# An attention and expert kernel: scatters of three batches in groups of three, gating operations moved behind the step's maximum

## The chip, the cores and the metric

The kernel runs on one core of a Trainium2 chip. The metric is the device time of one execution in microseconds (us). The core has five queues that run beside each other, each in its own program order: TensorE (PE; its weight loads are shown as PEld), VectorE (DVE), ScalarE (ACT), GpSimd (POOL) and the DMA issue of SyncE (SP). They wait for each other by semaphores.

## What is computed

Eight batches of 576 tokens go through an attention of eight heads (four with a local mask of 32, four with a strided one). The result, 4608 tokens of 512 numbers, goes through a layer of eight experts of which each token uses the one with the largest logit.

```python
scores = np.where(masks, scale * q @ k.T, -1e9)
attn = exp(scores - max) / (sum + 1e-9)
x = (attn @ v).transpose(0, 2, 1, 3).reshape(4608, 512)

logits = x @ w_gate
e_idx = np.argmax(logits, axis=1)
probs = softmax(logits)
gate_w = probs[np.arange(N), e_idx]
eom = 1.0 / (1.0 + np.exp(-(x @ w_output_gate)))
for e in range(E):
    mask = e_idx == e
    h = np.maximum(x[mask] @ w1[e], 0.0)
    out[mask] = gate_w[mask, None] * eom[mask, e, None] * (h @ w2[e])
```

## The kernel before

There are two stages. The attention stage has 40 steps, five for each batch, numbered t = 0 to 39, and then a tail (the second loop of `attention`) that drains what is left. The order on every queue is the order in which the program writes the instructions; nothing is reordered.

A step is a software pipeline over several step indices at once. In order: the scores of step t (`scores`, TensorE, L261 and L266), the normalisation of step t-4 in three parts (`norm`, VectorE, L347, L349, L352, whose result is x_t), the copy of turned rows of step t-5 (`evac_x`, ScalarE, L392 to L402), the rows' transfers to memory (`rows`, SP), the mask added (`bar`, VectorE, L279 or L284), the turned probabilities of step t-2 (`turn_p`, TensorE, L319) and their copy (`evac_p`, ScalarE, L325), the value matmuls of step t-3 (`values`, TensorE, L334 or L337), the row maximum (`top`, VectorE, L293), its subtraction (`shift`, GpSimd, L308), the turned rows of step t-4 (`turn_x`, TensorE, L383) and the exponential (`expo`, ScalarE, L312). The PSUM tiles of scores, of turned probabilities and of values have one buffer each.

Between these lie eight places, `pump(1)` to `pump(8)`: the first ahead of the second part of the normalisation, the second ahead of its third part, the third and fourth behind the maximum, its subtraction and the turned rows, the fifth to eighth behind the exponential. At each place every running chain puts out one further operation. A chain is a generator: `yield n` skips n places, and `yield 0, p` waits for place p. In the tail the places have no numbers, and a chain puts out its operations until one yields more than 0.

Each batch b has one chain for the second half of its logits, and at its end `gating`: the largest logit and its column `oh`, the sum of the exponentials (L550), the output logit of the chosen expert (L528, L531) and its sigmoid (L553, ScalarE), the slot numbers of the tokens (`numbers`, TensorE, L536 to L541; L592 and L595, VectorE), the count so far (`cum`, L589), and the gate weight (L597, L599, L602). Then come six scatters (L609, GpSimd), of 96 rows of 64 bytes each, into the `table` from which the experts' tokens are read. For batches 0 to 5 (`steady`) the chain lies in steps 5b+11 to 5b+13; batches 6 and 7 are gated in the tail. The scatters of batches 0 to 2 (`ci < EB - 1`, where EB is 4) begin two steps later. Behind the gating of batch 3 a chain `pick` (L453 to L466) chooses the first expert, and `ahead` loads its weights and gathers its first tokens.

The second stage runs the eight experts one behind another, on TensorE (L853, L873).

Of the kernel before, what the change touches and what calls it, by code (L numbers as in the profile page):

```python
# [34 lines left out]
EB = 4  # L35
# [20 lines left out]
def attn_moe_kernel(  # L56
# [21 lines left out]
    def distinct(ins, group):  # L78
        for other in group:
            tc.declare_no_dep(ins.ins, other.ins, reason="rows of one scatter are no rows of another")  # L80
        group.append(ins)
# [90 lines left out]
    def attention():  # L172
        with ExitStack() as actx:
# [276 lines left out]
            def pick():  # L450

                cp = ps_g.tile([128, 512], F32, name="gp")
                nc.tensor.matmul(out=cp[:, 0:E], lhsT=tri[0:QB, 1, :], rhs=cum[0:QB, EB, :], start=True, stop=True)  # L453
                yield 1
                nc.vector.scalar_tensor_tensor(out=pk[:, 0, :], in0=cp[:, 0:E], scalar=float(E), in1=wts,
                                               op0=ALU.mult, op1=ALU.add)
                yield 0
                nc.vector.tensor_reduce(out=pick_f, in_=pk[:, 0, :], axis=AX.X, op=ALU.max)
                yield 0
                nc.vector.tensor_tensor(out=first, in0=pk[:, 0, :], in1=pick_f.to_broadcast([128, E]), op=ALU.is_equal)  # L460
                yield 0
                nc.vector.tensor_tensor(out=pk[:, 1, :], in0=first, in1=eidx, op=ALU.mult)
                yield 0
                nc.vector.tensor_reduce(out=pick_f, in_=pk[:, 1, :], axis=AX.X, op=ALU.add)
                yield 0
                nc.vector.tensor_copy(out=pick_i, in_=pick_f)  # L466
# [47 lines left out]
            def gating(b, j0, j1, ci):  # L514
                n = j1 - j0
                steady = ci < HALVED - 1
# [10 lines left out]
                def output_logit():  # L527
                    V.tensor_tensor(out=dd[:, 2], in0=oh, in1=l[:, :, E:2 * E], op=ALU.mult)  # L528

                def output_sum():  # L530
                    R(out=f[:, 3, :], in_=dd[:, 2], axis=AX.X, op=ALU.add)  # L531

                def numbers():
                    pp_ = ps_g.tile([128, 512], F32, name="gp")
                    pv = pp_[0:QB, 0:n * E]
                    nc.tensor.matmul(out=pv, lhsT=tri[0:QB, 0, 0:QB], rhs=oh.rearrange("p j e -> p (j e)"),  # L536
                                     start=True, stop=False)
                    nc.tensor.matmul(out=pv, lhsT=tri[0:QB + 2, 1, 0:QB],
                                     rhs=cum[:, ci, :].unsqueeze(1).to_broadcast([QB + 2, n, E]), start=False, stop=False)
                    for j in range(n - 1):  # L540
                        nc.tensor.matmul(out=pp_[0:QB, E * (j + 1):E * n], lhsT=tri[0:QB, 1, 0:QB],  # L541
                                         rhs=oh[:, j, :].unsqueeze(1).to_broadcast([QB, n - 1 - j, E]),
                                         start=False, stop=(j == n - 2))
                    return pv

                def counts():
                    R(out=s8, in_=oh.rearrange("p j e -> p e j"), axis=AX.X, op=ALU.add)

                def exp_sum():
                    R(out=f[:, 2, :], in_=dd[:, 1], axis=AX.X, op=ALU.add)  # L550

                def sigmoid():
                    nc.scalar.activation(out=f[:, 4, :], in_=f[:, 3, :], func=AF.Exp, scale=-1.0)  # L553
# [13 lines left out]
                if steady:  # L567
                    counts()
                    yield 0
                    exp_sum()  # L570
                    yield 0, 1
                    pv = numbers()
                    output_logit()
                    yield 0
                    output_sum()
                    yield 0
                    sigmoid()
                else:
                    output_logit()
                    yield 0  # L580
                    output_sum()
                    yield 1
                    sigmoid()
                    pv = numbers()
                    counts()
                    yield 0
                    exp_sum()
                    yield 0
                V.tensor_tensor(out=cum[0:QB, ci + 1, :], in0=cum[0:QB, ci, :], in1=s8, op=ALU.add)  # L589
                yield 0 if steady else 1  # L590
                dst = dpool.tile([QB, n], I32, name="dst")
                V.tensor_tensor(out=dd[:, 3], in0=pv.rearrange("p (j e) -> p j e", j=n), in1=oh, op=ALU.mult)  # L592
                yield 0
                with nc.allow_low_precision(reason="one slot's number among zeros, written as an integer"):
                    R(out=dst, in_=dd[:, 3], axis=AX.X, op=ALU.add)  # L595
                yield 0, 1
                V.tensor_scalar(out=f[:, 4, :], in0=f[:, 4, :], scalar1=1.0, scalar2=None, op0=ALU.add)  # L597
                yield 0
                V.scalar_tensor_tensor(out=f[:, 5, :], in0=f[:, 2, :], scalar=1e-9, in1=f[:, 4, :],  # L599
# [4 lines left out]
                    rank()  # L604
                if ci == EB - 1:
                    chains.append([pick(), clock[0] + 1, None])
                yield 18 if ci < EB - 1 else 2
                for j in range(n):
                    i = nc.gpsimd.indirect_dma_start(  # L609
                        out=table[:, :], out_offset=bass.IndirectOffsetOnAxis(ap=dst[:, j:j + 1], axis=0),  # L610
                        in_=meta[:, b * NB + j0 + j, :], in_offset=None,
                        bounds_check=E * SLOTS - 1, oob_is_err=False)
                    distinct(i, scatters)
                    for r in early:
                        tc.declare_no_dep(i.ins, r.ins, reason="the slots read were all given by earlier batches")
                    yield 3
                if ci == EB - 1:
                    yield from ahead()

# [71 lines left out]
            while t < ns:  # L691
# [3 lines left out]
                b, j = t // NS, t % NS  # L695
# [453 lines left out]
```

## Time and profile before

| | us |
|---|---|
| median of three runs | 663.45 |
| lowest, highest | 660.99, 663.8 |
| the profiled execution's own time | 659.32 |
| its span, first to last instruction | 657.7 |
| attention stage with its tail | to about 200 |

The profile shows one execution. Busy times by engine over the whole span: TensorE 614.4 (93%), VectorE 293.7 (45%), ScalarE 276.8 (42%), GpSimd 185.7 (28%). These are averages over two stages with different limits, so the stages are read apart. In a timeline row the first number is the start, the second the duration, and a bracket tells how long the engine had been idle before and what released it; "remote" and "another core or an unknown queue" mean that the profile has no name for the releaser. "issue" is time in which the engine waited for nothing that the profile shows.

### The profile page before, as it was taken

To read this page: it belongs to the slowest core of one execution; us is meant where nothing else is said; L and a number is where in the kernel's file an instruction comes from. 1 tells how busy PE (TensorE), PEld (TensorE's weight loads), DVE (VectorE), ACT (ScalarE), POOL (GpSimd) and SP (SyncE) were. 2 spreads that over 40 slices of the span, in tenths; PEclk is the share of its full clock that TensorE was granted. 3 is DMA by queue.
4 is the path that set the end of the run, shared out by engine and by line. 5 is a ranking of instruction groups with operands and counts; after the bars stand their busy time and mean duration, and the time that the engine had idled before them with its cause. 6 is when DMAs were issued, how large, how long until landed. Compare 5 with 4: busy or idle time off the path is not lost.

```text
span 657.7 us, 14862 instructions
## 1 busy us (share of the span) xinstructions
PE 614.4 (93%) x5909; PEld 520.0 (79%) x5909; DVE 293.7 (45%) x645; ACT 276.8 (42%) x533; POOL 185.7 (28%) x194
## 2 busy tenths in 40 slices
PE   8889888888579999999999999999999999999995
PEld 6666666666348888988899899889988978988984
DVE  5877667775347223433153324234433422541500
ACT  3877766666225224433243333234234324433410
POOL 4334447565333402301220140024024013111011
PEclk9999999999888999999999999999999999999998
DMA  9998878794132724315223433245134054261001
GB/s 316 322 309 272 279 252 261 232 323 111 53 129 82 232 87 159 85 70 182 95 77 107 170 125 112 80 130 167 65 106 147 21 191 134 62 208 48 1 14 42
DMA packets 45536, 96.33 MB, mean 146 GB/s; under 512 B 8898, under 2 KB 20438, under 8 KB 45466
## 3 DMA queue, kind: packets, MB, share of 16 engines
q1 hardware_dynamic: 36010, 71.95, 33.5%
q0 software_dynamic: 8048, 20.05, 9.4%
q10 hardware_dynamic: 1408, 3.38, 1.5%
q8 instruction: 47, 0.77, 0.5%
q14 instruction: 23, 0.19, 0.1%
HBM read 75.85 MB, written 20.35 MB: 146 GB/s over the span
## 4 chain that ended last, share of the span: by engine, by line
PE 68%; issue 15%; DVE 6%; DMA 3%; POOL 3%; another core or an unknown queue 2%; ACT 2%; SPq 0%; POOLq 0%; DVEq 0%; ACTq 0%
PE yp L873 26%; PE hp L853 25%; PE tp L843 2%; PE xp L334 2%; PE xtp L383 2%; PE tp L319 2%; DMA raw<-in_moe_w_dram 2%; PE sp L501 2%; PE yp L897 1%; POOL out_dram L917 1%; PE sp L261 1%; PE xp L337 1%; PE sp L266 1%; POOL p_t L308 1%
## 5 line engine op out<-in xcount | busy, mean ns | idle before, releaser
L853 PE MATMUL hp<-xh,w1l 128*128 128x256 f32 (+1 forms) x480 | 147.9, 308 | 0.0
L853 PE MATMUL hp<-xl,w1h 128*128 128x256 f32 (+1 forms) x480 | 147.8, 308 | 0.0
L853 PE MATMUL hp<-xh,w1h 128*128 128x256 f32 (+1 forms) x480 | 147.7, 308 | 0.0
L917 POOL DMA_INDIRECT out_dram<-ys,tab x36 | 38.3, 1064 | 248.9 <-ACT ys L916 237.8
L853 PEld LDWEIGHTS hp<-xh,w1h 128*128 128x128 f32 x480 | 91.1, 190 | 1.9
L853 PEld LDWEIGHTS hp<-xl,w1h 128*128 128x128 f32 x480 | 91.0, 190 | 1.9
L853 PEld LDWEIGHTS hp<-xh,w1l 128*128 128x128 f32 x480 | 90.9, 189 | 1.4
L782 DVE TENSOR_TENSOR xl<-tp,xh 128x512 fp32r<-128x512 f32 (+3 forms) x40 | 25.7, 650 | 102.7 <-ACT xh L781 102.7
L873 PE MATMUL yp<-w2h,hhb 128*128 128x512 f32 (+1 forms) x176 | 71.0, 404 | 0.0
L858 ACT ACTIVATE hhb<-hp 128x384 fp32r<-128x384 f32 (+3 forms) x64 | 29.3, 459 | 98.1 <-PE hp L853 91.0
L861 DVE SCALAR_TENSOR_TENSOR hlb<-hp,hhb 128x384 fp32r<-128x384 f32 (+3 forms) x64 | 33.0, 516 | 84.0 <-ACT hhb L858 39.9
L781 ACT CAST xh<-tp 128x512 fp32r<-128x512 f32 (+3 forms) x40 | 21.8, 556 | 114.3 <-PE tp L843 114.3
L873 PE MATMUL yp<-w2l,hhb 128*128 128x512 f32 (+1 forms) x176 | 69.6, 396 | 0.0
L873 PE MATMUL yp<-w2h,hlb 128*128 128x512 f32 (+1 forms) x176 | 69.1, 393 | 0.0
L308 POOL TENSOR_TENSOR p_t<-p_t,st 128x512 f32<-128x512 f32 x40 | 42.6, 1066 | 71.2 <-DVE st L293 27.3
L609 POOL DMA_INDIRECT table<-meta,dst x48 | 44.5, 927 | 28.6 <-DVE f L563 12.1
L873 PE MATMUL yp<-w2h,hha 128*128 128x512 f32 x128 | 51.9, 405 | 0.0
L873 PE MATMUL yp<-w2l,hha 128*128 128x512 f32 x128 | 50.3, 393 | 0.0
L873 PE MATMUL yp<-w2h,hla 128*128 128x512 f32 x128 | 50.2, 392 | 0.0
L157 POOL DMA_INDIRECT xg<-xd,tab x40 | 45.5, 1136 | 15.6 <-issue 13.2
L861 DVE SCALAR_TENSOR_TENSOR hla<-hp,hha 128x256 fp32r<-128x256 f32 x56 | 23.6, 422 | 56.1 <-ACT hha L858 56.1
L916 ACT ACTIVATE ys<-yp,tab 128x512 f32<-128x512 f32 (+3 forms) x40 | 26.7, 666 | 48.4 <-issue 28.8
(149 smaller groups left out, 1041.1 us busy)
## 6 DMA issues: line engine op xcount, KB each, us to landing
raw<-in_moe_w_dram SPq DMA_DIRECT2D x54, 512.0 KB
vst<-in_vs_dram SPq DMA_DIRECT2D x8, 780.0 KB
vlt<-in_vl_dram SPq DMA_DIRECT2D x16, 292.5 KB
q_t<-in_ql_dram SPq DMA_DIRECT2D x8, 576.0 KB
q_t<-in_qs_dram SPq DMA_DIRECT2D x7, 650.0 KB
xd<-x_t SPq DMA_DIRECT2D x80, 54.0 KB
xd<-x_t SPq DMA_DIRECT2D x16, 256.0 KB
raw<-in_moe_w_dram ACTq DMA_DIRECT2D x6, 512.0 KB
```

The source lines that it names most:

```text
L157: nc.gpsimd.indirect_dma_start(out=dst, out_offset=None, in_=src, in_offset=bass.IndirectOffsetOnAxis(ap=idx, axis=0), bounds_check=top, o ...
L308: nc.gpsimd.tensor_tensor(out=p_t, in0=p_t, in1=st, op=ALU.subtract)
L319: nc.tensor.transpose(out=tp[:, w, i, :], in_=p_t[:, w, i], identity=ident)
L609: i = nc.gpsimd.indirect_dma_start(out=table[:, :], out_offset=bass.IndirectOffsetOnAxis(ap=dst[:, j:j + 1], axis=0), in_=meta[:, b * NB + ...
L781: nc.scalar.copy(out=hi, in_=src)
L782: nc.vector.tensor_tensor(out=lo, in0=src, in1=f32(hi), op=ALU.subtract)
L853: nc.tensor.matmul(out=hp[:, 0:n], lhsT=w[:, k, 128 * j:128 * (j + 1)], rhs=x[:, k, 0:n], start=first, stop=(k == KC - 1 and w is w1l))
L858: nc.scalar.activation(out=hh[:, j, 0:s], in_=hp[:, 0:s], func=AF.Relu)
L861: nc.vector.scalar_tensor_tensor(out=hl[:, j, 0:s], in0=hp[:, 0:s], scalar=0.0, in1=f32(hh[:, j, 0:s]), op0=ALU.max, op1=ALU.subtract)
L873: nc.tensor.matmul(out=yp[0:m, :], lhsT=h[:, j, o:o + m], rhs=w[:, j, :], start=(j == 0 and q == 0), stop=(j == FC - 1 and q == 2))
L916: nc.scalar.activation(out=ys[0:m, 0:n], in_=yp[0:m, 0:n], func=AF.Copy, scale=f32(tab[:, 1:2]))
L917: i = nc.gpsimd.indirect_dma_start(out=out.rearrange("t (k d) -> (t k) d", k=k), out_offset=bass.IndirectOffsetOnAxis(ap=row, axis=0), in_ ...
```

## The change

For the batches 0 to 5 the output logit (L528) moves from the first place of step 5b+12 to the third, ahead of the count (fourth). Its sum (L531) moves from the second to the fifth place, the sigmoid and L592 to the sixth, L595 to the seventh. In step 5b+13 the three operations of the gate weight (L597, L599, L602) move from the first, second and third place to the third, fourth and fifth. Behind batch 3, `pick` begins two places later with them.

The scatters of batches 0 to 2 come at the sixth and eighth place of step 5b+15 and the second of 5b+16, then at the sixth and eighth of 5b+16 and the second of 5b+17. Before, they came at the sixth place and the next step's second, three times, from step 5b+15 to the second place of 5b+18. The scatters of the other batches keep their places.

```diff
@@ gating @@
                     exp_sum()
                     yield 0, 1
                     pv = numbers()
+                    yield 0, 3
                     output_logit()
                     yield 0
-                    output_sum()
-                    yield 0
-                    sigmoid()
                 else:
...
                 V.tensor_tensor(out=cum[0:QB, ci + 1, :], in0=cum[0:QB, ci, :], in1=s8, op=ALU.add)
                 yield 0 if steady else 1
+                if steady:
+                    output_sum()
+                    yield 0
+                    sigmoid()
                 dst = dpool.tile([QB, n], I32, name="dst")
...
-                yield 0, 1
+                yield 0, 3
                 V.tensor_scalar(out=f[:, 4, :], in0=f[:, 4, :], scalar1=1.0, scalar2=None, op0=ALU.add)
...
-                yield 18 if ci < EB - 1 else 2
+                late = ci < EB - 1
+                yield 16 if late else 0 if steady else 2
                 for j in range(n):
                     i = nc.gpsimd.indirect_dma_start(
...
-                    yield 3
+                    yield (1, 1, 3, 1, 1, 3)[j] if late else 3
```

## Rows read from the trace of the kernel before

**Rows 1.** Busy us (x instructions) by stretch: PE, PEld, DVE, ACT, POOL, clock, DMA.

```profile
60.00:80.00 20.00, 17.44 (x393) 12.85 (x390) 14.84 (x48) 14.06 (x29) 11.33 (x12) 1.00 0.83 264
240.00:300.00 60.00, 60.00 (x351) 51.86 (x350) 23.90 (x36) 23.01 (x46) 11.55 (x11) 1.00 0.34 112
```

**Rows 2.** The chain that ended last: start, us, engine, tile and line.

```profile
64.52 0.13 issue
64.65 1.08 PE xp L334 x29
...
113.15 0.89 issue
...
123.45 3.02 DMA xd<-x_t
...
146.15 0.45 DVE dd L528
...
149.31 0.76 DVE f L597
```

**Rows 3.** Timeline of VectorE: steps 16 to 17, step 28, the tail.

```profile
62.50 0.21 DVE L565 TENSOR_TENSOR oh<-ew,f 96x48 bf16<-96x48 f32 x1
...
63.08 0.59 DVE L528 TENSOR_TENSOR dd<-oh,l 96x48 f32<-96x48 bf16 x1
...
63.71 0.20 DVE L531 TENSOR_REDUCE f<-dd 96x6 f32<-96x48 f32 x1
63.82 0.69 DVE L352 TENSOR_TENSOR x_t<-xp,rs 128x512 f32<-128x512 f32 x1
...
111.89 0.87 DVE L460 TENSOR_TENSOR first<-pk,pick_f 128x8 f32<-128x8 f32 x1
...
113.21 0.69 DVE L352 TENSOR_TENSOR x_t<-xp,rs 128x512 f32<-128x512 f32 x1
...
167.38 0.20 DVE L528 TENSOR_TENSOR dd<-oh,l 96x48 f32<-96x48 bf16 x1
```

**Rows 4.** Timeline of GpSimd: steps 15 to 18, and scatters in the tail.

```profile
59.94 1.01 POOL L609 DMA_INDIRECT table<-meta,dst  x1 [0.16 <-issue]
...
62.53 1.08 POOL L308 TENSOR_TENSOR p_t<-p_t,st 128x512 f32<-128x512 f32 x1 [0.35 <-DVE st L293]
...
66.06 1.04 POOL L308 TENSOR_TENSOR p_t<-p_t,st 128x512 f32<-128x512 f32 x1
67.26 0.92 POOL L609 DMA_INDIRECT table<-meta,dst  x1 [0.15 <-issue]
68.49 0.93 POOL L609 DMA_INDIRECT table<-meta,dst  x1 [0.30 <-issue]
...
169.95 0.92 POOL L609 DMA_INDIRECT table<-meta,dst  x1 [5.04 <-DVE meta L602]
...
174.86 0.92 POOL L609 DMA_INDIRECT table<-meta,dst  x1 [0.30 <-issue]
```

**Rows 5.** Two lines' instructions: durations in ns, minimum, median and maximum; shapes.

```profile
L528 DVE TENSOR_TENSOR dd<-oh,l x9: 180/531/595, 44.1 to 188.1; 96x48 f32<-96x48 bf16 x7, 96x24 f32<-96x24 bf16 x2
L597 DVE TENSOR_SCALAR f<-f x9: 154/168/833, 48.3 to 190.5; 96x6 f32<-96x6 f32 x7, 96x3 f32<-96x3 f32 x2
```

**Rows 6.** Timeline of ScalarE: steps 17 and 18, and the tail.

```profile
65.92 0.59 ACT L325 COPY pt<-tp 128x512 f32<-128x512 f32 x1 [0.93 <-PE tp L319]
...
68.07 0.63 ACT L312 ACTIVATE p_t<-p_t 128x512 f32<-128x512 f32 x1
...
70.58 0.59 ACT L325 COPY pt<-tp 128x512 f32<-128x512 f32 x1 [1.42 <-remote]
...
177.65 0.59 ACT L392 COPY xt<-xtp 128x512 f32<-128x512 f32 x1 [5.71 <-remote]
```

**Rows 7.** Timeline of VectorE: the maximum of steps 9, 14 and 29.

```profile
35.23 0.69 DVE L293 TENSOR_REDUCE st<-p_t 128x8 f32<-128x512 f32 x1
...
54.47 0.69 DVE L293 TENSOR_REDUCE st<-p_t 128x8 f32<-128x512 f32 x1
...
114.53 0.69 DVE L293 TENSOR_REDUCE st<-p_t 128x8 f32<-128x512 f32 x1
```

## What is predicted, and how

> **What bounds the kernel now.** I read the busy times by stretch first. In the attention stage (60 to 80 us) TensorE counts as busy 17.4 of 20 us, but VectorE 14.8, ScalarE 14.1 and the DMA engines 0.83 are close behind: no engine is alone in front, so what counts is the chain from one to the next. In the expert stage TensorE is busy all the time [rows 1]. The change touches only the attention stage; what the last attention step gains comes through to the end, since the experts' work starts behind it.
>
> Second, the chain of work that ended last, in the attention stage. I number the steps by their maximum (line 293), the first being step 0. Batch b has its scattered logits gated in steps 5b+11 to 5b+13: the output logit L528 stands in step 5b+12 and L597 in 5b+13. Through batches 0 to 3 the chain runs on TensorE and has small holes at the value matmuls, which wait for x_t (L352): x_t ends at 63.82 + 0.69 = 64.51, L334 begins 0.14 later, and TensorE had been free since 64.52 [rows 2, 3]. From 123 us on the chain runs through a row transfer (3.02 us) and then through VectorE, with L528 and L597 on it [rows 2].
>
> Third, the VectorE and GpSimd queues. L528 takes 0.59 us at 63.08, beside the shift (L308) that GpSimd runs from 62.53 to 63.61, and ends with it; in the tail, where no shift runs, the same shape takes 0.20 [rows 3, 4]. Its median over nine is 0.531; L597 has a median of 0.168 and a maximum of 0.833 [rows 5]. The Trainium skill ("SBUF — State Buffer", section "Who interferes with whom") says that a VectorE instruction with two SBUF inputs contends with a GpSimd instruction that reads SBUF, and that the one that starts first blocks the other for its whole length. The rows agree when GpSimd is first: the 0.59 ends with the shift.
>
> **The change, part by part.** Worked out from the order of the yields, eight places to a step:
>
> (a) *L528 from the first place of step 5b+12 to behind the maximum, L531 from the second to the fifth.* In the chain of steps 12, 17, 22 and 27, x_t comes up to 0.5 us sooner, but TensorE can use only its own hole, 0.13 us [rows 2]: 4 x 0.13 = 0.5 us gained (bounds 0 and 0.5).
>
> (b) *The choice of the first expert (pick) moves back by two places.* Its comparison L460 takes 0.87 us beside a shift and pushes x_t to 113.21; that ends at 113.90, and TensorE stands idle for 0.89 until 114.05 [rows 2, 3]. In its new place it lies behind the reciprocal of the next step, where the shift has 0.2 to 0.3 us left. Of 0.87 - 0.20 = 0.67 I take 0.4 (bounds 0 and 0.67).
>
> (c) *Steps 37 and 38.* Here the chain is VectorE's own: L528 with 0.45 and L597 with 0.76 lie on it [rows 2]. Ahead of x_t go L528 and L531 (0.45 + 0.11), and a step later L597 and L599 (0.76 + 0.11); behind the maximum come L528 and L531 again at 0.20 + 0.11. The 0.11 is the pitch of such small operations when nothing holds them (L531 at 63.71, the next at 63.82) [rows 3]. 1.43 - 0.31 = 1.1 us gained (bounds 0 and 1.1).
>
> (d) *Steps 32 and 33.* The same, but x_t of step 32 waits for its buffer's transfer (3.02 us, to 126.47) anyhow [rows 2], which hides L528. Left is 0.87 - 0.31 = 0.56 us, and behind it the chain goes into weight loads. I take 0.3 (bounds 0 and 0.56).
>
> (e) *Two-input operations behind the maximum.* They now start just before the shift and can hold it. The nearest row is L565, which already stands in that place: it runs 62.50 to 62.71, and the shift that is recorded from 62.53 takes 1.08 instead of 1.04 [rows 3, 4]. Two steps of six batches: 12 x 0.04 = 0.5, of which I count 0.4, as some of these shifts are not on the chain. By the page's rule taken whole, the shift would stand until 62.71, 0.18 each, 2.2 us in all; the row decides for 0.04, and 2.2 stays as the other end.
>
> (f) *The sigmoid behind the exponential on ScalarE, the reciprocal behind L599.* Both have a step until they are needed: nothing. If that cover went, a sigmoid costs 0.21 us.
>
> (g) *Scatters.* Before: two ahead of each of the shifts of steps 5b+16, 17 and 18 (b = 0, 1, 2). After: three ahead of the first two. On GpSimd's queue one follows the other by 1.23 us [rows 4]. From 59.94 on, the third ends at 59.94 + 2 x 1.23 + 0.92 = 63.32, and the shift of step 16 starts at about 63.47 instead of 62.53: 0.94 late. It ends at 64.55, the next three run from 64.71 to 68.09, and the shift of step 17 starts at 68.23 instead of 66.06: 2.17 late. Behind the shift stand the exponential L312 and, on ScalarE's queue, the copies of the next step. In step 17 these copies were done at 65.92 - 0.93 = 64.99 and ScalarE then waited for TensorE until 65.92 [rows 6]; 0.94 later fits into that to a hundredth. The exponential of step 17 goes from 68.07 to 69.29, its copies from 70.58 - 1.42 = 69.16 to 70.38, and ScalarE waited until 70.58 [rows 6]. So the late shift is hidden by waits for TensorE, and I take 0. Without that cover it costs 0.94 + 1.22 = 2.2 us in each of three batches, 6.5 in all. No other transfer hangs on these scatters: the table is first read behind batch 3.
>
> Sum: -0.5 - 0.4 - 1.1 - 0.3 + 0.4 = **-1.9 us**. Against the profiled execution (span 657.7, its own time 659.32) this gives 657.4. That execution is 4.1 us below the median of the runs, so against the median: 663.45 - 1.9 = **661.5**.
>
> **The rivals.**
>
> *A pause goes (faster).* The wait that ends at 70.58 has no releaser that the profile can name, and the same holds for five scatters in a row in the tail: they run from 169.95 to 175.78, and ScalarE's copy waits until 177.65 [rows 4, 6]. (177.65 - 169.95) / 5 = 1.54 us a scatter; for the pair at 67.26, (70.58 - 67.26) / 2 = 1.66. It looks as if TensorE's results came late until a group of scatters is through. After the change no scatter falls into step 18, and the group is through 1.3 us sooner (68.09 against 68.49 + 0.93 = 69.42). What can be won is bounded by the length of five steps: 54.47 - 35.23 = 19.24 without scatters, (114.53 - 54.47) / 3 = 20.02 with them [rows 7]; 3 x 0.78 = 2.3 us at most. With the sum: -4.2, 659.2 us. For it speaks how the ends fit; against it, that the number of scatters stays.
>
> *Three in a row pause longer (slower).* By 1.55 a scatter, the second group that starts at 64.71 is through at 69.4. If TensorE stands from step 17 until then, the work that lay between ScalarE's two waits, 69.16 - 65.92 = 3.24 us [rows 6], is still ahead, and step 18's copy comes at 72.6 instead of 70.58: 2.0 us x 3 = 6.0, less 1.9, +4.1: 667.6. It decides once TensorE stands longer behind the second group than in its two pauses of before, 0.93 + 1.42 by ScalarE's waits. Against it: in the tail ScalarE still got TensorE's results until 177.65 - 5.71 = 171.94, 2 us into a group [rows 6].
>
> *The late shift loses its cover (slower).* If the pauses shrink but the shift stays late, (g) costs up to 6.5: +4.6, 668.1. It needs ScalarE to wait less than the 0.93 of before.
>
> *The gain is lost (no change).* If from step 29 on the row transfers and weight loads set the pace, (b), (c) and (d) go, and (a) is left against (e): -0.1, 663.3. The 3.02 us in the chain speak for it.
>
> **How the numbers follow.** The forecast gets 0.50, the lost gain 0.16, the pause that goes 0.20, the longer pause 0.10, the late shift 0.04. A measurement of this kernel can tell about 0.5% (3.3 us) from no change; its runs spread over 2.8 us. Faster by more than that: 0.20 and 0.04 of the forecast's own tail, 0.24. Slower: 0.10 + 0.04 = 0.14. Within it: 0.62. The forecast's own bounds are all gains at their most and (e) at 0 (-0.5 - 0.67 - 1.1 - 0.56 = -2.8) and no gain with (e) at 2.2: 660.6 to 665.6. The range reaches down to the pause that goes, 659.2, and 0.7 below it for the spread of a median: 658.5 to 665.6; it leaves out the two slower cases, 0.14.
>
> **What would show it.** In the profile after: L528 near 0.2 us in all batches and L597 no longer at 0.8; the value matmuls of steps 12, 17, 22 and 27 right behind the transposes of L319; three scatters 1.23 us apart, and the shifts of steps 16 and 17 about 0.9 and 2.2 us behind their maximum's end instead of 0.2; ScalarE's wait ahead of L325 in step 17 near zero instead of 0.93. The five-step lengths from step 14 on tell the rivals apart: 20.0 as before for the forecast, near 19.2 for the pause that goes, 21.9 or more for the slower ones. The forecast is wrong if L528 in its new place still takes 0.5 us, or holds the shift for its whole length, or if ScalarE's wait ahead of L325 stays while the shift is late.

## The result, and the profile after

The changed kernel takes **670.69 us** (median of four runs, 670.10 to 672.98), where the kernel before took 662.31 beside it (660.99 to 663.80): a ratio of 1.0143, interval 1.0119 to 1.0168, so it is slower. The forecast was 661.5 with a range up to 665.6. Here and below medians are of all runs, ratios of the runs in the fast state alone. The profiled execution has a span of 669.3 us instead of 657.7, with a mean granted clock of 0.975 instead of 0.988.

Where the 11.6 us come from is read first from the starts of the row maximum (L293), which count the steps:

| us between starts of L293 | before | after | difference |
|---|---|---|---|
| steps 9 to 14 (gating, no early scatters) | 19.24 | 17.06 | -2.2 |
| steps 14 to 29 (three batches with early scatters) | 60.06 | 75.29 | +15.2 |
| steps 29 to 39 | 43.30 | 42.51 | -0.8 |
| step 39 to the end | 499.9 | 499.4 | -0.5 |

(Spans are compared here: the profiled execution of before lies 3 us below its median, so they differ by 11.6 where the medians differ by 8.4.) All the loss lies where the moved scatters are, and there in steps 17, 22 and 27: 8.74, 8.18 and 9.06 us, 5.2, 3.9 and 5.5 us longer than before. Windows of the kernel before over steps 14 to 29 (columns as in [rows 1]):

```profile
54.47:114.53 60.06, 51.78 (x1196) 38.70 (x1185) 44.78 (x134) 41.21 (x85) 33.83 (x35) 1.00 0.82 261
```

The same steps of the changed kernel, and behind them 6.8 us out of the first of the three batches:

```profile
52.06:127.35 75.29, 60.91 (x1188) 44.93 (x1181) 44.41 (x132) 41.74 (x85) 34.19 (x35) 0.86 0.70 226
...
65.70:72.50 6.80, 5.53 (x65) 3.98 (x64) 3.93 (x13) 2.84 (x5) 1.04 (x1) 0.50 0.78 261
```

TensorE does the same matmuls (1188 and 1196 are recorded), but is busy for 60.91 us instead of 51.78, +9.13, and idle for 14.38 instead of 8.28, +6.10. Together that is the 15.2. The other engines' busy times differ by at most 0.53 us. The clock's mean is 0.86, so 75.29 x 0.14 x 2 = 21 us ran at the lower of the two levels (0.50, or 1.2 GHz), one stretch of 6.8 us in each batch. Before, the clock was never low here.

The longer busy time is only in part the clock. Two other executions with the same groups of three, one of the scatters-alone kernel and one of the changed kernel again (both below), kept the full clock through their first batch. Steps 14 to 19 (the first batch) in windows: before, changed, scatters alone, changed again:

```profile
54.47:73.90 19.43, 17.05 (x406) 12.77 (x399) 14.45 (x43) 13.01 (x27) 10.90 (x11) 1.00 0.86 270
...
52.06:76.10 24.04, 20.05 (x402) 14.66 (x398) 14.62 (x43) 14.07 (x30) 10.85 (x11) 0.86 0.81 272
...
56.16:78.29 22.13, 18.05 (x402) 13.00 (x398) 14.68 (x43) 13.49 (x29) 10.87 (x11) 1.00 0.76 233
...
53.19:75.37 22.18, 18.42 (x407) 13.02 (x400) 14.51 (x44) 13.66 (x29) 10.88 (x11) 1.00 0.83 274
```

At the full clock the batch is already 2.7 us longer than before, and TensorE counts as busy for 1.0 to 1.4 us more, since the stops cut its work into small portions (four matmuls of L266 by themselves count 0.35 us, as shown below; 32 in one go count 0.69 in the kernel before). The low clock adds 1.9 us. Against this profile of before the clock is thus the smaller part of the 4.6 us. The sizes are of single executions, and rough: with pairs and at the full clock the gating-alone kernel took 21.44 us for this batch.

What precedes the low clock shows in the chain that ended last, changed kernel, steps 16 to 18 (answers to [rows 2]):

```profile
62.78 0.49 PE tp L319 x4
63.27 0.37 PE xp L334 x6
63.64 0.26 issue
63.90 0.39 PE xp L334 x3
64.28 1.04 issue
65.32 0.43 PE xp L334 x3
65.75 1.27 issue
67.02 1.54 PE xp L334 x20
68.55 1.05 PE xtp L383 x4
69.60 1.87 PE sp L261 x32
71.47 1.05 PE tp L319 x4
```

In the middle of the value matmuls of one step TensorE stops three times, for 0.26, 1.04 and 1.27 us, and waits for nothing that the profile shows. From 65.7 on, before the last of these stops ends, the clock is at 0.50: four transposes of L319 take 1.05 us in the chain at 71.47, and took 0.49 at 62.78. Beside it GpSimd's timeline of the changed kernel (answers to [rows 4]; the scatters are now on L612):

```profile
57.50 1.01 POOL L612 DMA_INDIRECT table<-meta,dst  x1 [0.16 <-issue]
58.81 0.93 POOL L612 DMA_INDIRECT table<-meta,dst  x1 [0.30 <-issue]
60.04 0.92 POOL L612 DMA_INDIRECT table<-meta,dst  x1 [0.30 <-issue]
60.97 1.06 POOL L308 TENSOR_TENSOR p_t<-p_t,st 128x512 f32<-128x512 f32 x1
62.20 0.92 POOL L612 DMA_INDIRECT table<-meta,dst  x1 [0.17 <-issue]
63.43 0.92 POOL L612 DMA_INDIRECT table<-meta,dst  x1 [0.31 <-issue]
64.65 0.92 POOL L612 DMA_INDIRECT table<-meta,dst  x1 [0.30 <-issue]
68.83 1.04 POOL L308 TENSOR_TENSOR p_t<-p_t,st 128x512 f32<-128x512 f32 x1 [3.26 <-DVE dd L528]
```

ScalarE's timeline of the changed kernel, the copy of turned probabilities in step 17 (answers to [rows 6]):

```profile
67.31 0.59 ACT L325 COPY pt<-tp 128x512 f32<-128x512 f32 x1 [3.88 <-remote]
```

The scatters follow each other by 1.23 us, as forecast. The second group begins at 62.20; 62.20 + 3 x 1.55 = 66.85, and TensorE goes on at 67.02. ScalarE has waited 3.88 us there. In the other two batches the same sum gives 90.79 and 115.64, and TensorE goes on at 90.73 and 115.33. The second shift of the first batch isn't late, 0.17 us behind the end of its maximum: GpSimd itself waits 3.26 us, since everything behind TensorE is late.

The gating operations did what was forecast (all instructions of L528 in the changed kernel: count, min/median/max ns, first and last start; answers to [rows 5]):

```profile
L528 DVE TENSOR_TENSOR dd<-oh,l x9: 178/194/204, 46.2 to 200.0; 96x48 f32<-96x48 bf16 x7, 96x24 f32<-96x24 bf16 x2
```

And the group of the shifts (L308) on GpSimd, busy us and mean ns of one:

```profile
L308 POOL TENSOR_TENSOR p_t<-p_t,st 128x512 f32<-128x512 f32 x40 | 42.5, 1063 | 83.2 <-DVE st L293 23.0 <-DVE dd L528 14.4 <-ACT pt L325 13.2
```

L528 has a median of 194 ns where it had 531 [rows 5], and a shift takes 1063 ns on average; over all 40 of the kernel before it was 1066. In step 17 the value matmuls (63.27) follow the transposes of L319 (62.78 + 0.49) without the hole of before.

### The profile page after: what moved, and what is told of

Read it like the earlier page. It is cut to its first block, busy times and chain, and to the rows that moved or that the text cites. A ratio compares the mean times of both kernels' runs of the same rounds, so it can differ in the third digit from the quotient of the medians.

```text
span 669.3 us, 14862 instructions
## 1 busy us (share of the span) xinstructions
PE 620.2 (93%) x5909; PEld 524.9 (78%) x5909; DVE 292.6 (44%) x645; ACT 277.4 (41%) x533; POOL 186.8 (28%) x194
## 4 chain that ended last, share of the span: by engine, by line
PE 69%; issue 16%; DVE 4%; ACT 3%; DMA 3%; POOL 3%; another core or an unknown queue 2%; SPq 0%; POOLq 0%; DVEq 0%; ACTq 0%
PE yp L876 25%; PE hp L856 25%; PE xtp L383 3%; PE xp L334 3%; PE tp L846 2%; PE tp L319 2%; PE sp L261 2%; PE sp L501 2%; PE xp L337 1%; PE yp L900 1%; POOL out_dram L920 1%; PE sp L266 1%; DMA ecst<-in_ecst_dram 1%; PE gp L415 1%
## 5 line engine op out<-in xcount | busy, mean ns | idle before, releaser
L308 POOL TENSOR_TENSOR p_t<-p_t,st 128x512 f32<-128x512 f32 x40 | 42.5, 1063 | 83.2 <-DVE st L293 23.0
L612 POOL DMA_INDIRECT table<-meta,dst x48 | 44.3, 923 | 29.0 <-DVE f L563 11.8
L157 POOL DMA_INDIRECT xg<-xd,tab x40 | 47.0, 1174 | 15.6 <-issue 13.5
```

The source lines that it names most:

```text
L157: nc.gpsimd.indirect_dma_start(out=dst, out_offset=None, in_=src, in_offset=bass.IndirectOffsetOnAxis(ap=idx, axis=0), bounds_check=top, o ...
L308: nc.gpsimd.tensor_tensor(out=p_t, in0=p_t, in1=st, op=ALU.subtract)
L612: i = nc.gpsimd.indirect_dma_start(out=table[:, :], out_offset=bass.IndirectOffsetOnAxis(ap=dst[:, j:j + 1], axis=0), in_=meta[:, b * NB + ...
```

## The experiments

The theories after the result: **hold** (scatters in flight keep TensorE from going on, and in threes long enough that its clock falls), **late shift** (the shift that is pushed back by three scatters costs the time, as the prediction's third rival had it), **gating** (the moved VectorE operations cost it). In the kernels with fills, plain transfers, fewer rows or reads the table lacks rows, so of them steps 14 to 29 are read, not the experts' stage. These kernels also fill the tile of the experts' first tokens with zeros ahead of its gather (`nc.gpsimd.memset(xgs[c], 0.0)`, two fills of 0.5 us, in every profile behind step 29).

### Which part of the change: gating alone, scatters alone

Gating alone is the changed kernel with the old places of the scatters (its `yield 16`, two places less than before, only makes up for the two places by which the gate weight moved back):

```diff
-                    yield (1, 1, 3, 1, 1, 3)[j] if late else 3
+                    yield 3
```

> Gating operations moved as in the change, scatters two by two as before. The theory that the scatter groups hold TensorE's results until they are through: the gating alone is worth what was forecast, 1 to 2 us less than before (about 660.5), and the 15 steps from step 14 to 29 take about 60 us as before. The rival that the moved gating operations themselves cost the time (they hold the shift or come late): most of the 9 us stays, about 668 to 671.

Scatters alone is the kernel before with the new places:

```diff
-                yield 18 if ci < EB - 1 else 2
+                late = ci < EB - 1
+                yield 18 if late else 2
...
-                    yield 3
+                    yield (1, 1, 3, 1, 1, 3)[j] if late else 3
```

> Scatters of the first three batches in groups of three as in the change, gating operations where they were before. Scatter theory: slower than the changed kernel by the lost gain of the gating, about 672, with the long steps at 17, 22 and 27 again. Rival (gating): about 662, as before.

Gating alone: 660.7 us, ratio 1.000, interval 0.9972 to 1.0028; the kernel before took 661.26 beside it. Its steps 14 to 29 take 64.53 us, not the 60 expected, with the scatters where they were; so executions with pairs differ by 4.5 us there, and the 15.2 us between two profiles is a rough size. Scatters alone: 673.24, ratio 1.0171, interval 1.0150 to 1.0193; steps 14 to 29 take 74.63 us, and steps 17, 22 and 27 take 8.5, 8.4 and 9.1. The scatters alone cost 12.0 us by the medians, no less than the whole loss of 8.4; **gating** falls.

### Late shift or transfers: fills in place of scatters

```diff
-                    i = nc.gpsimd.indirect_dma_start(
...
+                    if late:
+                        nc.gpsimd.memset(xe[0:QB].rearrange('p k n -> p (k n)'), 0.0)
+                    else:
+                        i = nc.gpsimd.indirect_dma_start(
...
```

> The changed kernel with each of the 18 scatters of the first three batches replaced, in the same place of GpSimd's queue, by a fill of 96 x 1024 numbers in SBUF, estimated at about 0.95 us from the 1.05 us that a fill of 1152 took: GpSimd stays as busy and the shift comes as late, but no transfer goes out. This leaves the scatters of 18 x 96 tokens out. If the late shift is the cause, steps 17, 22 and 27 stay at 8 us or more and the time at about 670. If the transfers of the scatters are, steps 14 to 29 take 58 us or less and the time falls to about 653 to 658.

664.01 us in all, ratio 1.0032, interval 1.0000 to 1.0063: the 653 to 658 expected without transfers did not come. Steps 14 to 29 did fall, to 55.44 us, less than before, and steps 17, 22 and 27 take 3.14, 3.15 and 3.15; the rest is lost behind step 39 (509 us instead of 499.9), which isn't read here. GpSimd's timeline of this kernel, first batch:

```profile
62.45 1.08 POOL L308 TENSOR_TENSOR p_t<-p_t,st 128x512 f32<-128x512 f32 x1
63.47 2.96 POOL L614 MEMSET xe<- 96x1024 f32 x3
66.40 1.04 POOL L308 TENSOR_TENSOR p_t<-p_t,st 128x512 f32<-128x512 f32 x1
```

TensorE's timeline of it, the wait behind the fills:

```profile
68.73 0.44 PE L383 MATMUL xtp<-ident,x_t 128*128 128x128 f32 x2 [0.44 <-ACT xt L392]
```

Here the second shift is 0.97 us behind the end of its maximum (usually 0.17), and TensorE waits 0.44 us for ScalarE's copy. In the second batch it is the same (0.97 late, 0.44 of wait); in the third the wait is 1.13, but there the exponential stood behind a copy of ScalarE (L232) that waited for a transfer, and began 0.66 after its shift had ended. So on this chip a shift that is 1 us late costs some 0.4 us, not 5: **late shift** falls for this result, though the fills (2.96 us for three) make the shift less late than three scatters do (3 x 1.23). The scatters themselves cost the time, by their transfers or by GpSimd's work of sending them off; the fills have neither.

### Scatters singly

```diff
-                    yield (1, 1, 3, 1, 1, 3)[j] if late else 3
+                    yield 5 if late else 3
```

> The changed kernel with the six scatters of a late batch six places apart, one by one over four and a half steps, instead of in two groups of three. If a group holds TensorE's results until it is through and single scatters are through before TensorE needs it, the steps become even and the 15 steps take 58 to 59 us: about 657 to 659. If each scatter costs TensorE its 1.6 us wherever it stands, it is as before or slower, 662 to 672. By the late-shift theory: no shift is later than 1 us, so about 660.

662.78 us, ratio 1.0015, interval 0.9989 to 1.0042, and 62.19 us for steps 14 to 29, with the clock at 1.00 throughout: as the pairs, within what can be told. No gain from taking the pairs apart is shown. (They are six places apart in the program; on GpSimd's queue the second and third of the first batch still begin 1.23 us apart, at 62.68 and 63.91.)

### What of a scatter: rows, addresses, queue, number in a row

Four kernels ran once each, on another chip. The first halves the rows (`m_ = QB // 2 if late else QB`, and the scatter takes `dst[0:m_, j:j + 1]` and `meta[0:m_, ...]`); two replace the scatter by a plain transfer of the same 96 rows to spare memory, from SyncE's or GpSimd's queue; the last puts all six in a row (`yield 0 if late else 3`).

```diff
-                    i = nc.gpsimd.indirect_dma_start(
...
+                    if late:
+                        nc.gpsimd.dma_start(out=spare[:, b * NB + j0 + j, :], in_=meta[:, b * NB + j0 + j, :])
+                    else:
+                        i = nc.gpsimd.indirect_dma_start(
...
```

> The changed kernel with the scatters of the first three batches cut to the first 48 of their 96 rows, in the same places; the other half of these rows is left out. GpSimd's instruction is expected to stay near its 0.92 us. If the pause is made by the scatters' row transfers, one group is through in half the time (2.4 us instead of 4.8), the long steps 17, 22 and 27 fall from 8 to 9 us to under 6, and steps 14 to 29 take 57 to 62 us instead of 75. If it is made by GpSimd's work of sending one scatter off, whatever its rows, it stays at 70 to 75.

> The changed kernel with each late scatter replaced by a plain transfer of the same 96 rows of 64 bytes, issued on SyncE's queue to a spare place in memory; the scatters themselves are left out. If small rows to memory are enough to hold TensorE, whoever issues them, steps 17, 22 and 27 stay long (8 us) and steps 14 to 29 near 75. If it needs GpSimd's own transfer queue, these 15 steps fall to 55 to 58 us, as with no transfer at all (55.4).

> The same plain transfer of 96 rows of 64 bytes to a spare place, issued on GpSimd's queue in the place of each late scatter; the scatters themselves are left out. If GpSimd's transfer queue with rows of 64 bytes is the cause, and not the indirect addressing, steps 14 to 29 stay at 70 us or more. If the indirect form is, they fall to 55 to 58.

> The changed kernel with the six scatters of a late batch at six places running, from the sixth place of step 5b+15: five ahead of one shift, the sixth behind it. The theory that TensorE is starved until a group is through, 1.6 us for each scatter: one long pause per batch, from about 3 us into the group until 8 to 10 us after its start, with the low clock behind it: the 15 steps take 75 to 82 us, and the time is 670 to 677. If the cost came from the number of groups instead (two of three against three of two), one group would be cheaper: below 70 us.

On this chip the kernel before took 643.09 us, 2.8% less than on the others. Steps 14 to 29: 55.81 us with half the rows, 57.34 and 51.08 with plain transfers from SyncE and GpSimd, 63.29 with six in a row (times 639.41, 655.96, 635.09, 645.33). The pauses marked "issue" are missing here near the scatters, even with six in a row, so the question could not be answered on it. It raised another: do the chips differ? (Why SyncE's plain transfers gave the longest time in all stays open; it is one execution.)

So the changed kernel was run again with three of these on one chip:

> The changed kernel itself, a second time, beside the kernel before on this chip. If the scatters in threes hold TensorE on every chip alike, the ratio is again 1.012 to 1.017 and the tops of steps 14 and 29 lie about 75 us apart (before: 60). If the hold depends on the chip, as the runs with half, plain and six transfers on a chip where before took 643 us let one think, then on a chip of that kind the ratio is 0.99 to 1.005 and the two tops lie 52 to 60 us apart; on a chip of the other kind (before near 660 us) the ratio is 1.014 again.

> The changed kernel with only 48 of the 96 rows in each scatter of the first three batches (the other rows of the table stay unwritten). If the hold goes by rows, and this chip shows it, steps 14 to 29 take about halfway between 55.4 us (no transfers) and 75.3 us (all rows), some 65; if it goes by the scatter whatever its size, about 75. Where this chip shows no hold, 52 to 57 as in the run before of this kernel.

> The changed kernel with each scatter of the first three batches replaced by a plain transfer from GpSimd's queue of the same 96 rows to a spare memory (so the table lacks them). If the hold comes from addresses taken from a tile, steps 14 to 29 take about 51 to 56 us on any chip; if any transfer of 96 rows from this queue holds TensorE, about 75 on a chip that shows the hold.

> The changed kernel with the six scatters of each of the first three batches at six consecutive places. If each scatter in flight costs its own part and those behind one another add up, steps 14 to 29 take 75 us or more on a chip that shows the hold (three in a row already make the low clock); if only the number of groups counts, less than 70. Where the chip shows no hold, 63 as before.

This chip is of the first kind: before 660.24, changed 669.53, ratio 1.0142, interval 1.0095 to 1.0188. Steps 14 to 29 by windows, one row for each kernel. The changed kernel:

```profile
53.19:126.33 73.14, 59.87 (x1200) 43.66 (x1191) 44.32 (x132) 41.89 (x86) 34.22 (x35) 0.91 0.71 229
```

With 48 rows in a scatter:

```profile
54.88:128.87 73.99, 59.91 (x1193) 44.08 (x1183) 44.51 (x132) 41.37 (x84) 33.56 (x35) 0.86 0.67 213
```

With plain transfers from GpSimd's queue:

```profile
54.40:109.52 55.12, 49.81 (x1196) 38.35 (x1189) 43.58 (x133) 41.90 (x87) 26.54 (x35) 1.00 0.90 296
```

With six scatters in a row:

```profile
54.10:128.01 73.91, 60.08 (x1190) 44.41 (x1183) 44.42 (x133) 41.63 (x85) 34.25 (x35) 0.86 0.70 224
```

Half the rows hold TensorE as long as all of them (674.97 us in all, ratio 1.0226, interval 1.0161 to 1.0291), so between 48 and 96 rows the hold goes by the scatter and not by its rows or bytes. The same rows sent plainly from the same queue hold nothing: 55.12 us, clock 1.00, and 652.26 us in all, ratio 0.9882, interval 0.9824 to 0.9941. (One pause without a releaser, 1.53 us, begins at 58.49, ahead of the first of them at 59.61.) In the same execution TensorE does pause, for 0.41 and 0.54 us, at the first two scatters of batch 3 (105.61 and 106.91), which keep their addresses. So it is neither the queue nor the rows' traffic. What differs is that the addresses come from a tile, that the rows go to scattered places, and that GpSimd spends 0.92 us on a scatter and 1.52 on three plain transfers; these were not taken apart. Six in a row take what two groups of three take (674.00, ratio 1.0212, interval 1.0146 to 1.0277): neither "75 or more" nor "less than 70" came true, so no rule of addition follows.

### Sixteen rows, and a read by addresses; the other kind of chip

The last question was whether a few rows hold less, and whether a read by addresses holds as well. Both kernels ran twice, each time on a chip of the second kind (the kernel before near 640 us); the second time the changed kernel and the one before ran beside them. The scatter of 16 rows is that of 48 with 16 in place of `QB // 2`; the read is:

```diff
+                        nc.gpsimd.indirect_dma_start(
+                            out=spg[:, b * NB + j0 + j, :], out_offset=None,
+                            in_=table[:, :], in_offset=bass.IndirectOffsetOnAxis(ap=dst[:, j:j + 1], axis=0),
+                            bounds_check=E * SLOTS - 1, oob_is_err=False)
```

> The changed kernel with only 16 of the 96 rows in each scatter of the first three batches (the other rows of the table stay unwritten). If the hold is the same for any scatter whatever its rows, as the run with 48 rows shows, steps 14 to 29 again take 73 to 75 us (on a chip where before takes about 660 us); if it goes by rows once they are few, 56 to 60 us.

> The changed kernel with each scatter of the first three batches turned round: an indirect transfer by the same addresses that reads the 96 rows from the table into a spare tile (so the table lacks them). If any transfer by addresses from a tile holds TensorE, steps 14 to 29 take 73 to 75 us; if it is the writing to the table, 55 us as with plain transfers.

> The changed kernel once more, to have it on the same chip as the next three. On a chip where before takes about 660 us the ratio is 1.014 as in the two comparisons so far and steps 14 to 29 take 73 to 75 us. On a chip where before takes about 640 us, the run with 48 rows (639.4 there) lets one think that nothing is held: ratio 0.99 to 1.00, steps 14 to 29 in 55 to 57 us. If threes hold TensorE there too, as six in a row did, the ratio is 1.003 to 1.01 and the steps take 61 to 64 us.

> The kernel before, for its profile on this chip. On a chip of about 660 us steps 14 to 29 take 60 us (as in its first profile). On a chip of about 640 us: 55 to 57 us if the pairs hold nothing there.

> The changed kernel with only 16 of the 96 rows in each scatter of the first three batches (the other rows of the table stay unwritten), on the chip of the changed kernel. If the hold is a fixed part per scatter, steps 14 to 29 take the same time as in the changed kernel on this chip, within 1 us; if it goes by rows, they take less: on a chip of about 660 us, 56 to 60 instead of 73 to 75.

> The changed kernel with each scatter of the first three batches turned round into a read of the table into a spare tile by the same addresses (so the table lacks these rows), on the chip of the changed kernel. If any transfer by addresses from a tile holds TensorE, steps 14 to 29 take at least as long as in the changed kernel on this chip; if it is the writing to the table, about 55 us.

| second kind of chip | median, us | before beside it | steps 14 to 29, us |
|---|---|---|---|
| before | 636.51 (the profiled execution) | 640.29 | 52.85 |
| changed | 642.89 | 640.29 | 56.50 |
| 16 rows | 639.63; earlier 640.32 | 640.29; 640.90 | 55.12; 55.11 |
| reads | 640.93; earlier 644.17 | 640.29; 640.90 | 57.30; 61.66 |

Since no hold shows here, these runs don't answer what they were made for. They show something else. The changed kernel has a ratio of 1.0036 here, interval 0.9994 to 1.0078: not told from no change. The reads of the earlier comparison have 1.0042, interval 1.0012 to 1.0073. Yet steps 14 to 29 of the two profiles differ by 3.65 us (that of before, 52.85, is below the 55 to 57 expected), and the windows tell how. Changed:

```profile
52.25:108.75 56.50, 48.79 (x1184) 37.37 (x1180) 45.42 (x132) 40.57 (x85) 34.24 (x35) 1.00 0.91 296
```

Before, on the same chip:

```profile
53.73:106.58 52.85, 48.77 (x1192) 37.40 (x1184) 45.59 (x135) 40.89 (x85) 33.74 (x35) 1.00 0.91 298
```

TensorE is busy for the same time to 0.02 us, at the full clock; the whole difference is idle time. GpSimd's timeline of the changed kernel on this chip, first batch:

```profile
60.23 0.92 POOL L612 DMA_INDIRECT table<-meta,dst  x1 [0.30 <-DVE f L563]
61.17 1.05 POOL L308 TENSOR_TENSOR p_t<-p_t,st 128x512 f32<-128x512 f32 x1
...
64.84 0.92 POOL L612 DMA_INDIRECT table<-meta,dst  x1 [0.30 <-issue]
65.77 1.06 POOL L308 TENSOR_TENSOR p_t<-p_t,st 128x512 f32<-128x512 f32 x1
```

TensorE's timeline of the same execution, step 18 of the pipeline and its like in the next batch:

```profile
68.14 0.66 PE L383 MATMUL xtp<-ident,x_t 128*128 128x128 f32 x4 [1.61 <-ACT xt L392]
...
86.92 0.66 PE L383 MATMUL xtp<-ident,x_t 128*128 128x128 f32 x4 [1.13 <-ACT xt L392]
```

The maxima of steps 16 and 17 end at 60.11 and 63.27, so these shifts start 1.06 and 2.50 us behind them, where every shift of steps 16 and 17 before is at 0.17. In the second and third batch it is 0.17 and 1.64, and 0.45 and 1.91. TensorE waits 1.61, 1.13 and (third batch) 1.39 us for ScalarE's copy L392, which stands behind the exponential: 4.1 us, of which before has 0.42. That is the size of the difference. ScalarE's timeline of the changed kernel, the exponential of steps 17, 22 and 27, and what stands ahead of the first:

```profile
65.94 1.06 ACT L232 COPY vev<-vlt 64x1040 f32<-64x1040 f32 x1 [1.91 <-PE tp L319]
66.90 0.62 ACT L312 ACTIVATE p_t<-p_t 128x512 f32<-128x512 f32 x1
...
85.68 0.63 ACT L312 ACTIVATE p_t<-p_t 128x512 f32<-128x512 f32 x1 [1.30 <-POOL p_t L308]
...
104.45 0.63 ACT L312 ACTIVATE p_t<-p_t 128x512 f32<-128x512 f32 x1 [1.84 <-POOL p_t L308]
```

In the second and third batch ScalarE waits for the shift alone: that is **late shift**. In the first, its copy L232 ran until the exponential, as late as the shift (which ended at 66.83), so there the two causes can't be told apart. The other kernels fit, and the wait grows with the lateness: with 16 rows a scatter takes GpSimd 0.84 us instead of 0.92, the second shifts start 1.92, 1.79 and 1.74 behind their maxima, and the waits are 1.35, 1.28 and 1.34; with reads (0.96) it is 2.71, 2.54 and 2.70, and the waits are 1.73, 1.72 and 1.73. Six in a row on such a chip make the first shift over 3 us late and TensorE waits up to 2.79 (TensorE's timeline of that kernel):

```profile
67.64 0.66 PE L383 MATMUL xtp<-ident,x_t 128*128 128x128 f32 x4 [2.79 <-ACT xt L402]
```

Behind that wait too the clock fell to 0.50, in all three batches, for 3.4 us each. Whether a read, or a scatter of 16 rows, holds TensorE on a chip of the first kind was not seen and stays open.

## Why the prediction was wrong

**The step that failed is (g),** the scatters, taken at 0. The queue's sum was right: about 0.9 and 2.2 us behind the maximum forecast, 1.06 and 2.50 in the first batch on a chip where TensorE isn't held (0.17 and 1.64, 0.45 and 1.91 in the others). Where it is held, only the first shift was late (1.05), the second not at all (0.17). The cover was wrong. It consisted of ScalarE's waits for TensorE, 0.93 and 1.42 us [rows 6]. Where TensorE isn't held, the same copies of the kernel before start right behind ScalarE's own work, without a wait (its timeline there, steps 17 and 18):

```profile
64.02 0.61 ACT L325 COPY pt<-tp 128x512 f32<-128x512 f32 x1
...
68.26 0.58 ACT L325 COPY pt<-tp 128x512 f32<-128x512 f32 x1
```

So those waits go with the scatters' hold: what was to hide the late shift is what the change makes larger. Groups of three made the wait ahead of L325 in step 17 3.88 us instead of near zero, the prediction's own sign of being wrong, and the scatters alone cost 12.0 us where (g) took 0. Where the hold is missing, the cover is missing too, and the steps are 3.65 us longer over three batches in the profile, inside the "up to 6.5" that the third rival named.

**The rival "three in a row pause longer" is what happened** on the chips of about 660 us. Its place was right (the second group, ahead of step 18), and so was its price per scatter: 62.20 + 3 x 1.55 = 66.85 against 67.02, and within 0.31 us in the other batches. Its point of decision was passed: ScalarE waits 3.88 us behind the second group, more than 0.93 + 1.42. Its 2.0 us a batch was somewhat small: against the profile of before the stop costs 2.7 in the first batch at the full clock. What it lacked is the clock. With a stop TensorE runs 6.8 us at 1.2 GHz, and that adds 1.9 us to the first batch. With 1.9 more a batch the rival would have stood at 3 x (2.0 + 1.9) - 1.9 = +9.8 us, an estimate from these two sizes; measured are +8.4 by the medians. The profile of before could have put the question: in the tail, in the window of 170 to 190 us with the five scatters in a row and the first two of seven, its granted clock is 0.83 and TensorE is busy for 13.29 of 20 us.

Its chance of 0.10 looks low as well. The ends of the pauses fitted 1.55 us a scatter in two places (1.54 and 1.66, from [rows 4, 6]); the one row against it, that TensorE still delivered 2 us into a group, holds for the beginning of a group and not for its end: in the changed kernel the stops behind a first group are of 0.39, 0.76 and 1.19 us, those of a second group come to 2.5 to 2.8 us a batch.

**(a) to (d), the gating moves, -2.3 us.** L528 takes 0.19 us, and steps 9 to 14, which have no early scatters, are 2.2 us shorter in the changed kernel. But in other executions these five steps take 17.11 to 20.81 us, with the gating in its old place 18.00 to 20.63 and in the new one up to 20.81, so that is no proof. Much of this spread goes with a pause of TensorE without a named releaser between 46 and 49 us, 0.99 us in the profile of before and none in that of the changed kernel; it comes with either placement, up to 1.88 with the new one (below). In the two profiles of one chip, neither with such a pause there, the steps take 18.00 before and 17.36 after, one pair of executions. Alone, the moves give a ratio of 1.000 with 0.28% to either side: a gain of 1.9 us (0.29%) lies at its edge. So the size of these terms stays open.

**(e), the operations behind the maximum, +0.4.** Smaller than taken: the shift's mean is 1063 ns, before 1066, so nothing is lost. The moved L528 ends before the shift starts (68.76 and 68.83 in step 17). Of the gate weight's operations the second, which reads two inputs, runs from 73.12 to 73.28, across the start of the shift at 73.18, and that shift takes 1.04 us like the others. The Trainium skill ("SBUF — State Buffer", section "Who interferes with whom") lets such an operation contend with a GpSimd operation that reads SBUF, and lets the one that starts first block the other for its whole length, which it says of two-port operations. By that rule the shift would have been held until 73.28; the row shows nothing of it.

**(f)** Nothing in the chains of the changed kernel shows the sigmoid or the reciprocal: right.

**The range** had its upper end at 665.6, since it left out both slower cases as 0.14 together. The first of them came true on the chips near 660 us. The second shows on those near 640 us in the profiles' steps, while the whole time there isn't told from no change.

No complete version beat the kernel before: gating alone and single scatters stand at 1.000 and 1.0015. What there would be to win if the early scatters held nothing can only be estimated, since the kernel with plain transfers lacks rows: its steps 14 to 29 take 55.12 us, against 60.06 of before in another comparison, some 5 us or 0.7%.

## What to carry to other kernels

Before a wait is counted as cover, ask what causes it: if it comes from the thing that is moved, it is no cover but part of the cost. A stop of TensorE is priced with the clock behind it, and the price is read from executions with and without the low clock. Scatters by addresses from a tile don't belong in threes in a stage that TensorE bounds (pairs and single ones could not be told apart), and whoever measures such a stage does so on more than one chip.

## What the runs showed of the hardware

**Scatters hold TensorE on some chips.** In the three comparisons in which the kernel before takes 660 to 662 us, TensorE stops near scatters by addresses, as long with 48 rows as with 96; in three others, on three other chips (640 to 643 us), it doesn't, and steps 14 to 29 of the kernel before take 52.85 us instead of 60.06. No chip is known to have served in two of the six, so whether this is the chip or its state at the time is not shown. What inside the chip causes the stop is open too. One rival was not tested, that TensorE runs short of instructions. The profile lists DMA queues of kind "instruction" (two packets, 0.03 MB, from 60 to 75 us of the changed kernel). One of these packets ends at 67.04, where TensorE goes on at 67.02; in the other batches nothing matches so (TensorE goes on at 90.73 and 115.33, the packets there end at 89.77 and 115.96). No run shows whether they come late behind scatters. During the stop TensorE goes on by small portions at an even beat. Changed kernel, TensorE, third batch:

```profile
111.74 0.35 PE L266 MATMUL sp<-kbs,q_t 64*64 64x64 f32 x4 [0.50 <-issue]
112.44 0.36 PE L266 MATMUL sp<-kbs,q_t 64*64 64x64 f32 x4 [0.36 <-issue]
113.17 0.35 PE L266 MATMUL sp<-kbs,q_t 64*64 64x64 f32 x4 [0.36 <-issue]
113.90 0.52 PE L266 MATMUL sp<-kbs,q_t 64*64 64x64 f32 x6 [0.38 <-issue]
```

Four matmuls at a time, 0.70 to 0.73 us apart, and the profile names nothing that they wait for. A pause without a named releaser alone is no sign of a scatter: with plain transfers from SyncE, on a chip without the hold and ahead of the first scatter, TensorE's timeline has

```profile
48.95 0.30 PE L335 MATMUL xp<-vlt,pt 128*32 128x130 f32 x1 [1.88 <-issue]
```

**The clock falls with a stop of a few us.** It stays at 1.2 GHz for 6.8 us in each batch of the changed kernel, and for 3.4 us behind the waits of 2.52 to 2.79 us for ScalarE with six in a row. With gating alone, the pairs met a low clock in one of the three batches (mean 0.97 over steps 14 to 29). In the repeat of the changed kernel the first batch escaped (mean 0.91 instead of 0.86) with the same scatters, and the reads' waits of 1.73 us were followed by a low clock on one chip and not on the other. So the same stop isn't always followed by a low clock.
